# Last attention layer of a four-layer kernel: the sums of squares of a block's later queries and keys share one turn of a PSUM bank, and the next queries are loaded once theirs are stored

## The chip, the cores and the metric

One core of one Trainium2 chip runs the whole program. The metric is the time of one execution in device microseconds (us). Engines are named as in the profile: PE is TensorE (PEld its weight loads), ACT is ScalarE, DVE is VectorE, POOL is GpSimd, SP is SyncE, which in this kernel issues the DMA transfers.

## The reference, cut to what matters

```python
x = A_x                                   # 2048 tokens x 512
x = x + attention(layernorm(x), A_wqkv, A_wo, window of 256)   # layer 0
x = x + attention(layernorm(x), B_wqkv, B_wo, all keys)        # layer 1
x = x + attention(layernorm(x), A_wqkv, A_wo, window of 256)   # layer 2
x = x + attention(layernorm(x), B_wqkv, B_wo, all keys)        # layer 3
# attention: 32 heads of 16; softmax(q k^T / 4) v, heads joined, times wo
```

The words `attention` and `layernorm` stand for the reference's own functions. Layers 1 and 3 are full attention: every query sees all 2048 keys.

## The kernel before, in words

**Pieces.** Tokens are cut into four chunks `c` of 512 queries, heads into eight groups `qd` of four heads, and into four head tiles `t` of eight heads (two groups each). In layer 3 the outer loop is over `t`, then `c`; one pair (t, c) is called a block here, and a block has the two head groups `qd` = 2t and 2t+1. For each head group there are 16 steps `j`, one for each 128 keys (`attn_full`). So a block has 32 steps, and the layer 4 x 4 x 32 = 512.

**A step.** PE makes two score tiles `s` (128 keys x two heads x 512 queries, line 767), ACT takes the exponential of each into a tile `e` (line 771), and PE multiplies `e` with the values into the bank `acc[0]` (line 821), two steps later (`flush(2)`). There are three score banks in layers 1 and 3 (`ps_s` has two, `third` is the other). So PE can be at most three exponentials ahead of ACT.

**Order on PE.** PE's instructions run in the order in which the program writes them. Between the steps the program deals out side work (class `Side`, function `share`): a model clock `clock`, a budget per step, and `PH["free"]`, the model time before which no side work may start, decide how many matmuls of side work follow a step. The order on the other queues is made by the scheduler from when data are expected; SP too takes its instructions strictly in its order, and a waiting one holds up those behind it.

**Side work of layer 3.** It is dealt by blocks (`side3`): in block (t, c) the queries of the next chunk for the same head tile, `Q3(c+1, t)`, then the keys of this chunk for the next head tile, `K3(c, t+1)`; parts of the values (`upper`) before these for t below 2, and parts of the output projection (`O3`) behind them, which for c below 3 there are only in t = 2 and, without a `K3`, in t = 3. With c = 3 come `K3`, then the key shift and `Q3(0, t+1)`. All side work accumulates in one bank, `acc[1]` (function `bank`).

**The sums of squares.** Softmax is kept in range by a shift made of the squared lengths of queries and keys. After a projection (`project`) the squares `sq` of the low-precision result `sp` are made on POOL, and PE sums them over a head's 16 rows with one matmul by `hsum` (line 582, 32 rows of `acc[1]`: rows 32t to 32t+31, `quarters`). For queries DVE scales the sums into `m` (line 611), SP stores `m` into row 3 of each head's rows in the DRAM tensor `qs` (line 617), and only then can the group's query tile `qt` be loaded from `qs` (`load_q`, line 782), since that load reads the row too. For keys DVE takes a maximum into `km` (line 598). Both endings are put on the list `pend`, and `settle()` runs all that stand there. Before: every unit of side work, before its first matmul, settles what is pending and then puts `PH["free"]` 1.6 us ahead (`mms`, lines 386 to 389). At a block's end the rest is settled (line 1089).

**The loads.** A head group needs `qt` (256 KB) and two halves of the keys `kt` (512 KB each, three buffers). Within a block the second group is loaded at the first one's start. The next block's first group is loaded at the start of this block's last group if its `Q3` is done by then (lines 1060 to 1063), otherwise when the next block starts; the scheduler then moves the issues on SP forward to where their data and buffers are expected.

## Time and profile before

| | |
|---|---|
| median of 3 runs | 2648.05 us (2645.96 to 2651.32) |
| the profiled execution | 2648.76 us, its span 2647.0 us |
| PE busy | 2578.7 us, 97% of the span |
| ACT busy | 2384.4 us, 90% |
| DVE, POOL busy | 848.5 us (32%), 583.1 us (22%) |
| layer 3, stretch of its 1024 exponentials | 944.9 us |
| granted PE clock over the span | 0.996 |

A row of groups names the line, the engine, the operation, what it writes and reads, the shape and the count; behind the bar come the busy time, the mean length of one in ns, and the idle time of the engine ahead of them with what ended it. A row of the timeline gives the start, the length, the engine, the line and the count of like instructions in a row; where these have other engines' work between them, the length is from the first start to the last end. In a row of windows, after the stretch and its length, come busy time and count of each engine, then the granted PE clock, the DMA share and GB/s. Busy lengths overlap: an exponential is recorded from its start in the queue, so its own length can be more than the distance to the next one.

### The profile page before, as it was taken

The page shows a single profiled execution, that of the slowest core. Times are in us where ns is not written, and L with a number is a line of the kernel's source. Part 1 is how long each engine was busy: PE and PEld are TensorE (multiplying, and loading weights), DVE is VectorE, ACT ScalarE, POOL GpSimd, SP SyncE. Part 2 cuts the span into 40 slices and gives each one's busy share as a digit, 9 for nine tenths or more (in the row PEclk, how much of TensorE's full clock was granted, in tenths as well). Part 3 has the DMA queues.
Part 4 walks back from the last instruction along what each step waited for, and adds up shares of the span by engine and source line. Part 5 has one row for each costly group of instructions (what it writes and reads, how often), then busy time and mean ns, then how long its engine had stood idle before and what let it go on. Part 6 is the DMA issues. An engine that isn't in the chain of part 4 may idle for free.

```text
span 2647.0 us, 63239 instructions
## 1 busy us (share of the span) xinstructions
PE 2578.7 (97%) x26201; PEld 773.2 (29%) x26201; DVE 848.5 (32%) x1947; ACT 2384.4 (90%) x2725; POOL 583.1 (22%) x1215
## 2 busy tenths in 40 slices
PE   8999999999999999999999999999999999999998
PEld 3333344322222222222223444422222222222222
DVE  5746653112232223112216666211111111222222
ACT  5777665999999999999997787699999999999997
POOL 1889760000000000000006788000000000000000
PEclk9999999999999999999999999999999999999999
DMA  6878766223242234222425655423222233334543
GB/s 203 203 234 266 212 187 186 62 95 124 99 110 91 92 115 123 76 70 88 140 69 161 210 155 158 147 77 94 83 77 69 78 114 99 112 113 139 169 139 116
DMA packets 293185, 341.34 MB, mean 129 GB/s; under 512 B 105928, under 2 KB 199592, under 8 KB 288280
## 3 DMA queue, kind: packets, MB, share of 16 engines
q1 hardware_dynamic: 284376, 310.17, 38.9%
q0 software_dynamic: 8512, 27.04, 3.7%
q8 instruction: 207, 3.39, 0.5%
q14 instruction: 90, 0.74, 0.1%
HBM read 226.49 MB, written 96.99 MB: 122 GB/s over the span
## 4 chain that ended last, share of the span: by engine, by line
PE 86%; ACT 5%; DVE 4%; issue 2%; POOL 1%; DMA 1%; SPq 0%; ACTq 0%; DVEq 0%
PE acc L821 35%; PE s L767 23%; PE acc L395 11%; PE b L398 7%; PE acc L855 5%; ACT e L771 5%; PE b L395 3%; PE bs L398 2%; DVE ot L729 1%; POOL e L844 1%; POOL e L847 0%; DMA x<-in_A_x_dram 0%; DVE xh L462 0%; DVE xh L471 0%; DVE sp L558 0%
## 5 line engine op out<-in xcount | busy, mean ns | idle before, releaser
L771 ACT ACTIVATE e<-s 128x1024 f32<-128x1024 f32 (+2 forms) x2432 | 2246.4, 1086 | 104.5 <-PE s L767 89.6
L821 PE MATMUL acc<-e,vt 128*17 128x512 f32 x8192 | 1078.4, 598 | 4.9 <-DVE ot L729 3.6
L767 PE MATMUL s<-qt,kt 64*128 64x512 f16 (+3 forms) x5440 | 749.8, 354 | 21.4 <-ACT e L771 10.8
L767 PEld LDWEIGHTS <-kt 64*128 64x128 f16 x5440 | 191.1, 94 | 696.3 <-issue 679.3
L821 PEld LDWEIGHTS acc<-e,vt 128*17 128x17 f32 x8192 | 136.4, 95 | 394.7 <-issue 361.7
L729 DVE STREAM_TRANSPOSE ot<-acc 128x512 f32<-128x512 f32 x128 | 91.5, 715 | 496.2 <-PE acc L821 392.3
L847 POOL TENSOR_SCALAR_AFFINE_SELECT e<-e 128x256 f32<-128x256 f32 x512 | 233.6, 464 | 73.7 <-ACT e L771 72.6
L844 POOL TENSOR_SCALAR_AFFINE_SELECT e<-e 128x256 f32<-128x256 f32 x448 | 196.6, 446 | 42.2 <-ACT e L771 39.0
L855 PE MATMUL acc<-e,vt 128*17 128x384 f32 (+2 forms) x2816 | 197.5, 390 | 0.6 <-POOL e L844 0.5
L398 PE MATMUL b<-xc,w 128*128 128x512 f16 x520 | 125.4, 386 | 6.7 <-DMA xc<-xh 4.1
L671 DVE COPY vt<-acc 128x256 f32<-128x256 f32 (+1 forms) x48 | 23.6, 492 | 335.5 <-PE acc L395 335.5
L395 PE MATMUL acc<-wv,xc 128*32 128x256 f16 (+1 forms) x2304 | 120.6, 299 | 0.1
L395 PEld LDWEIGHTS <-xc 128*32 128x32 f16 x2688 | 77.0, 97 | 137.7 <-issue 132.9
L751 POOL TENSOR_TENSOR oh<-o,oh 128x512 f16<-128x512 f32 x19 | 22.1, 1162 | 432.0 <-DVE oh L750 428.8
L676 POOL TENSOR_SCALAR vt<-vt 128x16 f32<-128x16 f32 (+1 forms) x48 | 11.2, 233 | 462.9 <-DVE vt L671 462.7
L395 PE MATMUL acc<-xc,w 128*32 128x512 f16 x1344 | 107.9, 379 | 0.0
L395 PE MATMUL acc<-xc,w_h 128*32 128x512 f16 x1296 | 107.7, 379 | 0.0
L563 POOL TENSOR_TENSOR sq_h<-sp_h 128x512 bf16<-128x512 f16 x27 | 28.1, 1041 | 356.4 <-DVE sp_h L557 295.5
L563 POOL TENSOR_TENSOR sq<-sp 128x512 bf16<-128x512 f16 x28 | 29.2, 1041 | 349.0 <-DVE sp L557 349.0
L557 DVE TENSOR_SCALAR sp<-acc 128x512 f16<-128x512 f32 x28 | 19.4, 692 | 242.3 <-PE acc L395 242.3
L712 DVE SCALAR_TENSOR_TENSOR x<-acc,x 128x512 f32<-128x512 f32 x60 | 41.4, 690 | 169.4 <-PE acc L395 163.4
L395 PEld LDWEIGHTS <-w 128*32 128x32 f16 x1920 | 56.0, 97 | 115.3 <-issue 101.9
(165 smaller groups left out, 1749.4 us busy)
## 6 DMA issues: line engine op xcount, KB each, us to landing
kt<-kf SPq DMA_DIRECT2D x126, 512.0 KB
xd<-x SPq DMA_DIRECT2D x96, 256.0 KB
qt<-qs SPq DMA_DIRECT2D x96, 256.0 KB
x<-xd SPq DMA_DIRECT2D x96, 256.0 KB
w<-wd SPq DMA_DIRECT2D x16, 1024.0 KB
qs<-sp SPq DMA_DIRECT2D x48, 256.0 KB
wv<-wd SPq DMA_DIRECT2D x20, 512.0 KB
x<-in_A_x_dram SPq DMA_DIRECT2D x32, 256.0 KB
```

The costliest lines, as they stand in the source:

```text
L395: nc.tensor.matmul(ps[g:g + 32], a[:, g:g + 32], b, start=(i == 0), stop=(i == len(pairs) - 1), skip_group_check=True)
L398: nc.tensor.matmul(ps, a, b, start=(go and i == 0), stop=(i == len(pairs) - 1))
L563: nc.gpsimd.tensor_tensor(sq, sp[:, 0], sp[:, 0], ALU.mult)
L671: LAST["DVE"] = nc.vector.tensor_copy(to, fr).ins
L712: nc.vector.scalar_tensor_tensor(xs[i], ps, 1.0 / (UP[2] * UP[3]), xs[i], op0=ALU.mult, op1=ALU.add)
L729: nc.vector.transpose(ot.rearrange("p b r -> p (b r)"), a)
L767: nc.tensor.matmul(ps[:, h, s0:s0 + wd_], kt[R * h:R * h + R, pr, kc:kc + P], qt[R * h:R * h + R, pr, qc:qc + wd_], start=True, stop=True)
L771: LAST["ACT"] = nc.scalar.activation(e[:, :, w0:w1], ps[:, :, w0:w1], AF.Exp, scale=SCALE).ins
L821: nc.tensor.matmul(a[32 * h:32 * h + DH + 1, :], V[l, qd // 4, j // 8][:, j % 8, 4 * (qd % 4) + h, :], es_[h // 2][:, h % 2, :], start=(j ...
L844: last = nc.gpsimd.affine_select(v, v, pattern=[[0, 2], [-1, P]], compare_op=ALU.is_gt, fill=0.0, base=0, channel_multiplier=1)
L847: last = nc.gpsimd.affine_select(v, v, pattern=[[0, 2], [1, P]], compare_op=ALU.is_ge, fill=0.0, base=0, channel_multiplier=-1)
L855: nc.tensor.matmul(a[32 * h:32 * h + DH + 1, q * P:(q + nb) * P], V[l, (4 * c + j) // 4][:, j % 4, 4 * qd + h, :], es_[h // 2][:, h % 2, s ...
```

## The change

- `mms` no longer settles when exactly one ending is pending and it belongs to another head tile than the unit that is about to start (`hold`). So the endings of `Q3(c+1, t)` wait, `K3(c, t+1)` runs, and both are settled together: by the next unit of side work, or, where the block has none, at the block's end.
- Where nothing was pending ahead of such a unit, the model holds the next side work back by 1.5 instead of 2.2 after it.
- In the full layers `project` no longer settles by itself after its matmuls.
- The load of the next block's first group is no longer tried only once, at the start of the block's last group, with a forced settling; it is tried after each step of that group, and made when the queries are done and their ending is no longer pending. If that does not happen within the block, it is made when the next block starts, as before.

```diff
-    def mms(ps, pairs, after=1.45, us=MM, go=True):
+    def mms(ps, pairs, after=1.45, us=MM, go=True, hold=None):
...
-        if PH["full"] and pend:
+        if PH["full"] and pend and not (len(pend) == 1 and hold is not None and pend[0][3] not in (None, hold)):
             settle()
             PH["free"] = clock[0] + 1.6
             yield 0.1
...
                 ps = bank()
-                yield from mms(ps, [(w[:, k, a, w0:w0 + P], xc[:, b, k, :]) for k in range(NC) for a, b in TERMS], 2.2)
-            settle(not sqs)
+                yield from mms(ps, [(w[:, k, a, w0:w0 + P], xc[:, b, k, :]) for k in range(NC) for a, b in TERMS],
+                               1.5 if PH["full"] and ht is not None and not pend else 2.2, hold=ht)
+            if not PH["full"]:
+                settle(not sqs)
...
-        pend.append((clock[0] + 3.6, rest, None))
+        pend.append((clock[0] + 3.6, rest, None, ht))
...
-        pend.append((clock[0] + 3.6, rest, ("Q", l, c)))
+        pend.append((clock[0] + 3.6, rest, ("Q", l, c), ht))
...
-                    nxt = None
+                    nxt = following = None
                     if qd + 1 in qds:
                         nxt = load(l, c, qd + 1)
                     elif l == 3:
-                        b, u = (c + 1, t) if c + 1 < NQ else (0, t + 1)
-                        if u < NHT and ("Q3", b, u) in DONE and (b or ("H", u) in DONE):
-                            settle()
-                            loaded[b, 2 * u] = load(l, b, 2 * u)
+                        following = (c + 1, t) if c + 1 < NQ else (0, t + 1)
                     elif c + 1 < NQ and ("Q", l, c + 1) in DONE and (l == 1 or ("K", l, c + 1) in DONE):
-                        if any(f == ("Q", l, c + 1) for _, _, f in pend):
+                        if any(f[2] == ("Q", l, c + 1) for f in pend):
                             settle()
                         loaded[c + 1, qds[0]] = load(l, c + 1, qds[0])
...
                         sd.step()
+                        if following is not None:
+                            b, u = following
+                            if u < NHT and ("Q3", b, u) in DONE and (b or ("H", u) in DONE) and not any(f[2] == ("Q", 3, b) for f in pend):
+                                loaded[b, 2 * u] = load(l, b, 2 * u)
+                                following = None
```

What this does to the order of instructions shows first on PE in the first block of layer 3 (t = 0, c = 0). In a name such as `sq3_0_1_h0` stand the layer, 0 for queries or 1 for keys, the chunk and the head tile; in `e3_0_1_13` layer, chunk, head group and step; in `kt3_1_0_0` and `qt3_1_0` layer, chunk and head group (and the half). The last number is only a running one. Before, the squares of the next chunk's queries are summed in the middle of the second head group, behind the value products of its step 3:

```order
L821 MATMUL acc0_81<-e3_0_1_3_0_23157,vt3_0_0_21822 17x512 x2
L821 MATMUL acc0_81<-e3_0_1_3_1_23162,vt3_0_0_21822 17x512 x2
L582 LDWEIGHTS hsum_86
L582 MATMUL acc1_82<-sq3_0_1_h0_0_23175,hsum_86 32x512
L767 LDWEIGHTS kt3_0_1_0_22648
L767 MATMUL s3_0_1_6_0_23209<-qt3_0_1_22646,kt3_0_1_0_22648 128x512
```

Now they stand at the block's very end, with those of the keys, and the next PE instruction is the first score matmul of the next block, which reads the `qt` of these very queries (line numbers are those of the changed kernel, up to four higher):

```order
L823 MATMUL acc0_81<-e3_0_1_13_0_23358,vt3_0_1_22568 17x512 x2
L823 MATMUL acc0_81<-e3_0_1_13_1_23363,vt3_0_1_22568 17x512 x2
L584 LDWEIGHTS hsum_86
L584 MATMUL acc1_82<-sq3_0_1_h0_0_23175,hsum_86 32x512
L584 LDWEIGHTS hsum_86
L584 MATMUL acc1_82<-sq3_1_0_h1_1_23338,hsum_86 32x512
L769 LDWEIGHTS kt3_1_0_0_23406
L769 MATMUL s3_22643<-qt3_1_0_23404,kt3_1_0_0_23406 128x512
```

So the queries' sums moved from ten steps ahead of the block's end to its end. The same holds for the blocks with c = 0, 1, 2 of t = 0 and t = 1, six in all: there no unit of side work follows `K3` within the block. With t = 2 the two sums stand together in step 3 of the second group (ahead of `O3`), and in the other blocks they move by a step at most.

On SP, at the same place, the rows before are these; `m3_1_0` is the store of the shift row and `qt3_1_0` the load of the next block's queries, `kt3_1_1_0` a half of the keys for the next block's second group:

```order
L571 DMA qs1_1_102<-sp3_0_1_h0_0_23172 128x1024
L572 DMA qs1_1_102<-sp3_0_1_h0_0_23172 128x512
L617 DMA qs1_1_102<-m3_1_0_23206 8x512
L782 DMA qt3_1_0_23404<-qs1_1_102 128x2x512
L792 DMA kt3_1_0_1_23408<-kf_96 128x2x1024
L782 DMA qt3_1_1_23410<-qs1_1_102 128x2x512
L361 DMA wv3_0_1_0_23386<-wd1_2_111 128x8x256
L568 DMA kf_96<-sp3_1_0_h1_1_23339 128x2x512
L569 DMA kf_96<-sp3_1_0_h1_1_23339 128x512
L792 DMA kt3_1_1_0_23412<-kf_96 128x2x1024
```

And now:

```order
L573 DMA qs1_1_102<-sp3_0_1_h0_0_23172 128x1024
L574 DMA qs1_1_102<-sp3_0_1_h0_0_23172 128x512
L794 DMA kt3_1_0_1_23408<-kf_96 128x2x1024
L361 DMA wv3_0_1_0_23382<-wd1_2_111 128x8x256
L570 DMA kf_96<-sp3_1_0_h1_1_23335 128x2x512
L571 DMA kf_96<-sp3_1_0_h1_1_23335 128x512
L794 DMA kt3_1_1_0_23412<-kf_96 128x2x1024
L619 DMA qs1_1_102<-m3_1_0_23399 8x512
L784 DMA qt3_1_0_23404<-qs1_1_102 128x2x512
L784 DMA qt3_1_1_23410<-qs1_1_102 128x2x512
```

The store of `m` and the load of `qt` moved behind `kt3_1_1_0`, whose buffer is given up only by the last score matmuls of the block.

## The prediction, made before the changed kernel was run

> **What bounds the kernel now.** The change acts in layer 3 alone, so I read that stage first. The windows view of the stretch in which its exponentials run, one row for all engines, and the groups of that stretch:

> ```profile
> 1690.00:2625.00 935.00, 927.42 (x9057) 233.09 (x9060) 173.88 (x382) 932.88 (x1014) 50.09 (x62) 1.00 0.34 106
> L771 ACT ACTIVATE e<-s 128x1024 f32<-128x1024 f32 x1014 | 933.6, 1166 | 2.1 <-PE s L767 1.4
> ```

> The first number behind the length is PE, the fourth ACT. ACT is busy 932.9 of 935 us and its idle time in front of 1014 exponentials adds up to 2.1 us; PE is busy 927.4. Both are full, and ACT is the bound. How fast ACT can go shows in a stretch where nothing holds it, against the whole layer (the windows view, ACT's line 771 alone):

> ```profile
> 1924.66:2071.32 146.66, 146.66 (x161) 1.00 0.24 71
> 1687.10:2632.00 944.90, 942.73 (x1024) 1.00 0.34 105
> ```

> 160 exponentials (one of the 161 is cut by the edge) take 146.66 us, 0.917 us each. 1024 of them make 939 us; the layer takes 944.9. So whatever the change does to the order of side work, it can win at most about 6 us, and whatever keeps ACT without scores is lost one for one, since there is no slack to win it back.

> **What the change adds.** In six blocks the store of `m` and the load of `qt` now begin with sums of squares at the block's end, and the next PE instruction needs that `qt`. Before, they stood eight to twelve steps, 15 to 22 us, ahead of that end. The timeline before at such an end (first block):

> ```profile
> 1744.32 0.92 PE L767 MATMUL s<-qt,kt 64*128 64x512 f16 x4
> 1744.85 0.09 PEld L767 LDWEIGHTS <-kt 64*128 64x128 f16 x1 [0.42 <-issue]
> 1745.27 0.36 SPq L792 DMA_DIRECT2D kt<-kf  x1
> 1746.04 0.38 PE L582 MATMUL acc<-sq_h,hsum 128*32 128x512 bf16 x1
> 1746.35 0.39 PE L767 MATMUL s<-qt,kt 64*128 64x512 f16 x2
> ```

> The last two score tiles of the block are made from 1744.32; the second begins at about 1744.85, when ACT has given up a bank. With three banks ACT then has three exponentials left, 3 x 0.917 = 2.75 us, to 1747.60. The sums of squares stand at 1746.04. So from their start ACT is covered for 1.56 us. The squares' start is my zero below.

> How long the chain from squares to scores takes shows once in the trace, at the start of layer 3, where PE does wait for a `qt` (timeline):

> ```profile
> 1679.62 0.39 PE L582 MATMUL bs<-sq_h,hsum 128*32 128x512 bf16 x1
> 1680.05 0.68 DVE L611 TENSOR_SCALAR m<-bs 32x512 f16<-32x512 f32 x1 [1.74 <-PE bs L582]
> 1680.81 0.32 SPq L617 DMA_DIRECT2D qs<-m  x1
> 1683.73 0.37 SPq L782 DMA_DIRECT2D qt<-qs  x1
> 1686.60 0.82 PE L767 MATMUL s<-qt,ke 64*128 64x512 f16 x6 [0.82 <-DMA qt<-qs]
> 1687.09 5.60 ACT L771 ACTIVATE e<-s 128x1024 f32<-128x1024 f32 x6 [0.63 <-PE s L767]
> ```

> Squares to DVE 0.43, DVE 0.68, to the store's issue 0.08, `qt`'s issue to the score matmul 2.87, to the exponential 0.49. Between the two issues there stood other SP work here, so the store is better read elsewhere (SP's own rows, two places):

> ```profile
> 1728.59 0.29 SPq L617 DMA_DIRECT2D qs<-m  x1
> 1730.02 0.38 SPq L782 DMA_DIRECT2D qt<-qs  x1
> ...
> 1789.35 0.34 SPq L571 DMA_DIRECT2D qs<-sp_h  x1
> 1789.74 0.42 SPq L572 DMA_DIRECT2D qs<-sp_h  x1
> 1790.26 0.44 SPq L792 DMA_DIRECT2D kt<-kf  x1
> 1791.85 0.29 SPq L617 DMA_DIRECT2D qs<-m  x1
> 1794.60 0.89 SPq L782 DMA_DIRECT2D qt<-qs  x2
> ```

> Alone it takes 1.43 us until `qt` can be issued; with two `sp` stores and a 512 KB `kt` issued in the 2.5 us ahead, 2.75. In the changed order a `kt` stands right ahead of the store (0.77 us ahead of the squares, by the rows 1745.27 and 1746.04, so some 2 us ahead of the store), but no `sp` store is near. I take 1.8, nearer to the lone one, and keep 1.43 and 2.75 as ends.

> The chain: 0.43 + 0.68 + 0.08 + 1.8 + 2.87 = 5.86 us (5.49 to 6.81). ACT stands idle from 1.56 to 5.86 + 0.49, that is 4.79 us, and the first string after an idle time is 0.1 us longer (six exponentials in 5.60 against 6 x 0.917 = 5.50). **4.9 us per block end, six of them: 29.3 us** (27.1 to 35.0). The second group of squares reads no such chain; its wait for DVE to read the bank lies inside the gap, and so does the load of the second `qt`.

> **What PE does after such a gap.** PE idles from the second sums to 5.86, some 4 us. What that does to its clock shows at two places in the windows view (columns as above; behind the five engines stands the granted clock) and in the chain of waits:

> ```profile
> 300.00:304.00 4.00, 0.52 (x8) 0.00 (x0) 3.90 (x9) 0.26 (x1) 3.99 (x8) 0.93 1.08 341
> 304.00:307.00 3.00, 2.37 (x6) 0.87 (x7) 1.39 (x3) 0.00 (x0) 1.85 (x4) 0.50 1.05 430
> 330.90:334.30 3.40, 1.48 (x22) 0.66 (x24) 3.30 (x6) 0.24 (x1) 0.00 (x0) 1.00 0.62 237
> 334.40:337.60 3.20, 3.20 (x23) 1.44 (x14) 2.25 (x6) 2.12 (x3) 3.11 (x7) 0.50 0.70 181
> 368.50:371.80 3.30, 1.59 (x16) 0.65 (x19) 3.23 (x9) 1.09 (x3) 1.32 (x2) 1.00 1.01 206
> 371.90:375.30 3.40, 3.40 (x37) 1.26 (x33) 1.10 (x4) 2.36 (x4) 2.21 (x6) 1.00 0.98 270
> ```

> ```profile
> 304.63 5.28 PE b L398 x12
> 311.71 2.70 PE b L398 x12
> ```

> After 3.5 idle us of 4 the clock was 0.50, and twelve matmuls took 5.28 instead of 2.70. A stretch of 3.4 us in which PE was busy 1.48 (44%) was followed by about 3.2 us at half clock, one with 1.59 of 3.3 (48%) was not. In the new gap PE has 0.4 us of work in 4, so each gap should bring such a slow stretch. How much of it falls behind the gap depends on how the 3.4 us stretches lie: from 1.5 to 3.4 us, I take 2.8. PE loses half of it, 1.4 us, and since PE has no slack beside ACT (927 of 935), ACT loses it too: **6 x 1.4 = 8.4 us** (0 to 10.2).

> [...]

> **What it moves elsewhere.** In the three blocks of t = 2 both sums stand in the middle, and the second waits for DVE to have read the first (0.43 + 0.68 = 1.1 us). PE is up to three exponentials ahead there, so the wait is mostly covered: I take 0.5 each, 1.5 us (0 to 3.3). The loads there follow at once, some 12 steps ahead of their use: nothing. Some steps that stood empty of side work now hold some, since fewer pauses of 1.6 model us are made. Their price is bounded by the 6 us between 939 and 944.9, below nothing; most of it belongs to places the change leaves (the layer's start, the steps after a new group), and I take -1. What moved by one step in the other blocks costs nothing: the same matmuls run, covered by a full ACT.

> **Sum.** 29.3 + 8.4 + 1.5 - 1 = 38 us, on the profiled execution's 2648.8 (span 2647.0, 0.7 above the median of the runs shown): **2687 us**.

> **Rivals.**
> - *Half clock does not come, or seldom.* For it: at 368.5 a stretch with 1.7 idle us of 3.3 left the clock at 1.00. Against it: the new gaps are more than twice as long. Without the term: 2687 - 8.4 = 2679. Chance 0.2. [...]
> - *The keys' transfer holds the store and the queries.* `kt` is 512 KB on the same queue, and the 2.75 us above was measured behind one. Then the chain is 6.81 us, the stall 5.84, six times 0.95 more: 2693. `qt` too may land late behind it, which I bound by as much again: 2699. Chance 0.13.
> - *The wait is covered, and the fuller steps win.* This one ends on the other side. If the queries of the six ends were in place by the time ACT has used up its three tiles, nothing of the chain would count, and what is left is the gain of up to 6 us: 2643 to 2648. It decides where the chain is under 1.56 - 0.49, about 1.1 us. Against it: the load alone took 2.87. It would need the load to be issued ahead of the block's end, as in t = 2, and the SP rows of the changed order show it behind `kt3_1_1_0`. That the change does less than it says (loads "when stored") is in this order too: stored late, the queries are loaded late. Chance 0.03.

> **Numbers.** The forecast has 0.64. Its own bounds are 27.1 + 6 + 0 - 3, with 2678, to 35.0 + 10.2 + 3.3, with 2697. To hold 8 in 10 the range takes in the first two rivals, less one end of each: 2674 to 2699. A measurement of this kernel can tell about 0.2%, 5 us, from no change: slower 0.97, the same 0.02, faster 0.01 (the last two share the third rival's chance, which lies mostly within 5 us).

> **What the changed profile would show.** Six idle times of ACT of 4 to 6 us ahead of line 771 (its idle time in this stretch 25 to 40 us instead of 2.1), put down to PE's line 767; PE's line 767 waiting for the DMA of `qt` six times; at each, squares, `m`, its store, `kt` ahead of it, `qt` in this order; the granted clock at 0.50 for about 3 us after each; the blocks' other stretches still at 0.917 us per exponential. It is wrong if `qt` is issued ahead of the last score matmuls of the block, if ACT's idle time stays below 10 us, or if the lost time lies in other blocks than these six.

## The result, and the profile after

The change makes the kernel slower: 2694.38 us median (2691.19 to 2695.85, six runs) against 2648.89 us (2644.59 to 2651.32, six runs) of the kernel before, a ratio of 1.0172 (95% interval 1.0161 to 1.0182). That is 45.5 us more, where the forecast said 38. The profiled spans are 2693.3 and 2647.0 us, 46.3 apart. Line numbers below are those of the changed kernel; the exponentials of line 771 now have line 773, the scores of 767 have 769.

The layer first. The windows view of the changed kernel, ACT's exponentials alone, over the stretch that answers to the row of 944.90 us before, then their group:

```profile
1687.20:2678.30 991.10, 947.01 (x1024) 0.99 0.33 101
```

```profile
L773 ACT ACTIVATE e<-s 128x1024 f32<-128x1024 f32 x1019 | 942.4, 1128 | 44.0 <-PE s L769 42.9
```

All of the 46 us is here: 991.1 against 944.9. ACT's idle time ahead of the exponentials rose from 2.1 to 44.0 us. In the waits view of the changed kernel (who waits for whom, us in total, times, longest) the first row is ACT's, and three rows of PE stand behind it:

```profile
ACT e L773 <- PE s L769: 42.9, 35, 4.8
PE s L769 <- DMA qt<-qs: 23.7, 6, 4.1
PE acc L584 <- DVE m L613: 7.0, 9, 0.8
PE acc L584 <- POOL sq_h L565: 3.5, 9, 0.4
```

PE waits six times for a `qt`, 4 us each, once at each of the six block ends. The list before had no such row. At the first of these ends the timeline of the changed kernel shows the chain (start, length, engine; SPq is an issue of SP):

```profile
1744.34 0.92 PE L769 MATMUL s<-qt,kt 64*128 64x512 f16 x4
1745.29 0.36 SPq L794 DMA_DIRECT2D kt<-kf  x1
1746.06 0.38 PE L584 MATMUL acc<-sq_h,hsum 128*32 128x512 bf16 x1
1746.48 0.68 DVE L613 TENSOR_SCALAR m<-acc 32x512 f16<-32x512 f32 x1 [5.41 <-PE acc L584]
1747.18 0.30 SPq L619 DMA_DIRECT2D qs<-m  x1
1747.21 0.39 PE L584 MATMUL acc<-sq_h,hsum 128*32 128x512 bf16 x1 [0.77 <-DVE m L613]
1748.78 0.87 SPq L784 DMA_DIRECT2D qt<-qs  x2
1751.52 1.03 PE L769 MATMUL s<-qt,kt 64*128 64x512 f16 x4 [3.92 <-DMA qt<-qs]
1752.22 1.94 ACT L773 ACTIVATE e<-s 128x1024 f32<-128x1024 f32 x2 [4.66 <-PE s L769]
1752.48 1.91 PE L823 MATMUL acc<-e,vt 128*17 128x512 f32 x8
1755.67 1.02 ACT L773 ACTIVATE e<-s 128x1024 f32<-128x1024 f32 x1 [1.51 <-PE s L769]
```

From the squares at 1746.06 to the scores at 1751.52 it takes 5.46 us: 0.42 to DVE, 0.68 on DVE, 0.02 to the store's issue, 1.60 from there to the issue of `qt`, 2.74 from there to the first score matmul; over the six ends it is 5.40 to 5.65. ACT stands 4.66 us, starts, does two exponentials, and stands again for 1.51 us at 1755.67. That second idle time is the half clock's, as keep_busy shows below. The windows view on PE's own slow stretches at two ends (busy time and count of PE, PEld, DVE, ACT, POOL, then the granted clock):

```profile
1747.39:1750.80 3.41, 0.21 (x1) 0.00 (x0) 0.68 (x1) 0.17 (x1) 0.00 (x0) 0.98 0.48 163
1750.80:1754.22 3.42, 2.71 (x16) 0.53 (x20) 0.00 (x0) 1.94 (x2) 0.00 (x0) 0.50 0.26 91
1754.20:1757.40 3.20, 3.20 (x28) 0.75 (x24) 0.00 (x0) 1.73 (x2) 0.00 (x0) 0.50 0.00 0
1757.60:1761.00 3.40, 3.40 (x54) 1.14 (x50) 2.81 (x8) 2.24 (x4) 0.15 (x1) 1.00 0.01 2
...
1815.65:1819.06 3.41, 0.00 (x0) 0.00 (x0) 0.58 (x1) 0.00 (x0) 0.00 (x0) 0.99 0.48 163
1819.06:1822.47 3.41, 2.95 (x20) 0.65 (x20) 0.00 (x0) 1.94 (x2) 0.00 (x0) 0.51 0.15 53
1822.50:1825.80 3.30, 3.30 (x44) 0.95 (x40) 1.47 (x6) 2.52 (x3) 0.00 (x0) 1.00 0.00 0
```

After the idle stretch at the first end the clock is 0.50 for 6.8 us, at the second for 3.4. Over the six ends it is 6.8 us twice and 3.4 us four times.

How much each place costs shows when the layer is cut into pieces of 32 exponentials (one block and head group: 16 steps of two), from the end of one piece's last exponential to that of the next. In the trace before, the 32 pieces take between 29.3 (32 x 0.917) and 30.3 us, and the first one, from its first start, 30.9. The six pieces that begin with a new block behind the six ends, in us:

| piece | before | after | more |
|---|---|---|---|
| t 0, c 1, first group | 29.33 | 36.98 | 7.65 |
| t 0, c 2 | 29.33 | 35.52 | 6.19 |
| t 0, c 3 | 29.33 | 36.56 | 7.23 |
| t 1, c 1 | 29.33 | 35.93 | 6.60 |
| t 1, c 2 | 29.33 | 35.61 | 6.28 |
| t 1, c 3 | 29.50 | 37.05 | 7.55 |

They hold 41.5 of the 46.2 us; 4.7 lie in other pieces.

### The profile page after: what moved, and what is told of

Its sections match the earlier page's. It is cut to its first block, busy times and chain, and to the rows that moved or that the text cites. A ratio compares the mean times of both kernels' runs of the same rounds, so it can differ in the third digit from the quotient of the medians.

```text
span 2693.3 us, 63244 instructions
## 1 busy us (share of the span) xinstructions
PE 2592.3 (96%) x26201; PEld 772.2 (29%) x26201; DVE 845.5 (31%) x1947; ACT 2389.3 (89%) x2725; POOL 583.1 (22%) x1215
## 4 chain that ended last, share of the span: by engine, by line
PE 84%; ACT 5%; DVE 5%; issue 2%; DMA 2%; POOL 1%; SPq 0%; ACTq 0%; DVEq 0%
PE acc L823 34%; PE s L769 22%; PE acc L395 11%; PE b L398 7%; PE acc L857 5%; ACT e L773 5%; PE b L395 3%; PE bs L398 2%; DMA qt<-qs 1%; DVE ot L731 1%; DMA xc<-xh 0%; DMA qs<-m 0%; POOL sq_h L565 0%; DMA x<-in_A_x_dram 0%; DVE sp_h L559 0%
## 5 line engine op out<-in xcount | busy, mean ns | idle before, releaser
L398 PE MATMUL b<-xc,w 128*128 128x512 f16 x520 | 125.3, 386 | 5.5 <-DVE oh L752 4.3
```

The costliest lines, as they stand in the source:

```text
L398: nc.tensor.matmul(ps, a, b, start=(go and i == 0), stop=(i == len(pairs) - 1))
```

## The experiments

Each is an edit of the changed kernel. Ratios are to the kernel before, run on the same chip. Its medians were 2647.15 us beside half_dose, hold_alone, keep_busy and sums_earlier, 2648.37 beside load_alone, keys_behind, pause_2_2 and middle_alone, and 2649.48 beside queries_first and middle_both_first; it was 2648.89 beside the changed kernel.

**half_dose: the deferred ending at three ends instead of six.** The queries' ending waits only for keys of head tile 1, that is in t = 0; everything else settles as before, and the model's pause is 2.2 as before.

```diff
-                               1.5 if PH["full"] and ht is not None and not pend else 2.2, hold=ht)
+                               2.2, hold=ht if ht == 1 and s == 1 else None)
```

> Only the three block ends of t = 0 keep the shared turn; all other blocks settle as before the change. If the time is lost in the chain from squares to the next block's first scores (theory A), three of the six ends remain, which cost 7.65, 6.19 and 7.23 us in the profile after: before + 21, about 2670 us. If it is lost by the new spread of the side work and the waits around the shared bank in all of the layer (theory B), the loss follows the changed blocks of all four head tiles and three of them leave about a quarter: about 2660 us.

2665.75 us, 1.0073 (1.0056 to 1.0089). The waits view of this kernel:

```profile
ACT e L773 <- PE s L769: 20.6, 13, 4.8
PE s L769 <- DMA qt<-qs: 11.8, 3, 4.0
```

The layer is 20.4 us longer than before, and the three pieces behind the three ends are longer by 7.58, 6.26 and 6.49, 20.3 us together; the three ends of t = 1 are at 29.33, 29.33 and 29.50 again. The total fell between the two expectations, so it is the pieces that decide: the loss sits at the ends, 6.8 us each, and goes where they go.

**hold_alone: the load tried once, as before, the ending deferred.** The new retry after each step is taken out.

```diff
-                        following = (c + 1, t) if c + 1 < NQ else (0, t + 1)
+                        b, u = (c + 1, t) if c + 1 < NQ else (0, t + 1)
+                        if u < NHT and ("Q3", b, u) in DONE and (b or ("H", u) in DONE) and not any(f[2] == ("Q", 3, b) for f in pend):
+                            loaded[b, 2 * u] = load(l, b, 2 * u)
```

> The shared turn without the repeated try of the load: the load of the next block's first group is tried once, at the start of the last group, and not while its ending is pending. Theory A: the six ends stay as they are, since there the ending is pending to the block's end in either form: 2694 us, within 3. If the repeated try had a part in it (the load placed badly), the time moves by more than 5 us.

2695.91 us, 1.0183 (1.0166 to 1.02): the whole of the loss, without the changed load.

**load_alone: the other half, the new load with the endings settled as before.**

```diff
-                               1.5 if PH["full"] and ht is not None and not pend else 2.2, hold=ht)
+                               2.2)
```

> The repeated try of the load without the shared turn (every unit settles what is pending, as before). PE's order is that of the kernel before. Theory A: no loss, 2649 us within 3. If the place from which the load is made matters, a few us either way.

2647.79 us, 0.9999 (0.9989 to 1.001). The pause is 2.2 here too, and pause_2_2 below keeps nearly the whole loss with that pause and the later ending. So the later ending is the cause; the rule for the load neither costs nor wins by itself.

**keep_busy: PE kept at work in the gap.** At the six ends PE is given 14 matmuls of constants into a part of the bank that nothing reads; the result doesn't use them.

```diff
+WARM = 14
...
                 if not win:
+                    idle = len(pend) == 2
                     settle()
+                    if idle:
+                        for _ in range(WARM):
+                            nc.tensor.matmul(acc[1][96:128], ones[:, :32], ones, start=True, stop=True, skip_group_check=True)
```

> The changed kernel with 14 more matmuls behind the shared sums at each of the six ends, into 32 rows of the second bank that nothing reads; they fill PE's gap from about 2.3 to 5.3 us behind the squares and add no work that the result uses. If the half clock behind the gap costs ACT about 2 us per end, the granted clock stays at 1.00 and the time falls by 10 to 13 us, to about 2682. If the slow stretch is covered and the loss is the chain alone, nothing changes: 2694, or a little more where the extra matmuls end late.

2684.08 us, 1.0142 (1.0125 to 1.0159): 10 us under the changed kernel by the medians, 8 by the ratios. Its timeline at the first end, then the windows view behind it:

```profile
1746.42 3.18 PE L1098 MATMUL acc<-ones 128*32 128x512 f16 x14 [0.77 <-DVE km L601]
1746.74 0.87 SPq L785 DMA_DIRECT2D qt<-qs  x2
1749.53 0.60 PE L770 MATMUL s<-qt,kt 64*128 64x512 f16 x4
1750.02 1.94 ACT L774 ACTIVATE e<-s 128x1024 f32<-128x1024 f32 x2 [4.41 <-PE s L770]
1750.07 1.05 PE L824 MATMUL acc<-e,vt 128*17 128x512 f32 x8
```

```profile
1749.50:1752.90 3.40, 3.40 (x43) 1.06 (x45) 0.00 (x0) 2.88 (x4) 0.00 (x0) 1.00 0.03 9
```

The chain is as long as ever (`qt`'s issue to the scores 2.79 us), ACT still stands 4.41 us, but the clock stays at 1.00; eight value products take 1.05 us instead of 1.91, and the second idle time is 0.19 us instead of 1.51. The six pieces are now 31.3 us longer than before instead of 41.5. The half clock is worth 10.2 us in this pair of traces, 1.7 per end, and what is left is 5.2 per end: 4.7 to 4.9 at the four ends with c = 1 and 2, 5.9 and 6.1 at the two with c = 3.

**sums_earlier: the queries' ending settled inside the block**, near the time at which the model expects the keys' squares; the keys' ending stays at the block's end. The queries' sums come out one step (1.8 us) ahead of the keys' at two ends and two steps (3.7 us) at four.

```diff
                             b, u = following
+                            if b and len(pend) == 2 and pend[-1][0] - 2.0 <= clock[0]:
+                                settle(True, 1)
+                                PH["free"] = clock[0] + 1.6
```

> The queries' sums are made one step (two ends) or two steps (four ends) ahead of the block's end, the keys' sums stay there; on SP the store goes ahead of the keys' transfer, the load of the queries stays behind it and so waits for the last score matmuls. Theory A: the load is issued about 0.3 us ahead of my zero instead of 2.7 behind it, so each end costs 2 to 3 us instead of 6.9: 2664 to 2670 us. Theory B, which puts the loss in the bank and the spread of the side work: these have not changed, so about 2694.

2690.93 us, 1.0168 (1.0151 to 1.0185): a miss. In this trace the layer starts 1.63 us earlier than in the changed kernel's (1685.62 against 1687.25). Counted from that start, the sums of the first end come 1.83 us earlier, the scores only 0.71. Its timeline at the first end:

```profile
1742.60 0.38 PE L584 MATMUL acc<-sq_h,hsum 128*32 128x512 bf16 x1
1743.72 0.30 SPq L619 DMA_DIRECT2D qs<-m  x1
1744.11 0.37 SPq L794 DMA_DIRECT2D kt<-kf  x1
1745.04 0.88 SPq L784 DMA_DIRECT2D qt<-qs  x2
1749.18 1.04 PE L769 MATMUL s<-qt,kt 64*128 64x512 f16 x4 [4.36 <-DMA qt<-qs]
1749.88 1.94 ACT L773 ACTIVATE e<-s 128x1024 f32<-128x1024 f32 x2 [3.94 <-PE s L769]
```

The 512 KB `kt`, whose buffer the last score matmuls free at about 1744, now goes out between the store and `qt`, and the scores come 4.14 us after `qt`'s issue instead of 2.74. At the four ends with two steps the order costs more. There `kt` waits for that buffer, and `qt`, behind it on SP, is issued 2.2 us after the store (1.3 at the first end); the scores then come 4.4 to 4.7 us after `qt`'s issue. The next two kernels test that reading.

**keys_behind: `kt` issued behind `qt`**, in the changed kernel's own place for the sums.

```diff
-        nc.sync.dma_start(qt, qs[1, c][2 * qd:2 * qd + 2].rearrange("r p n -> p r n"))
+        LQ[qd] = nc.sync.dma_start(qt, qs[1, c][2 * qd:2 * qd + 2].rearrange("r p n -> p r n")).ins
...
+            with tc.issue_after(LQ[qd - 1]) if l == 3 and qd % 2 and qd < 4 else nullcontext():
                 nc.sync.dma_start(kt, kf[pair, :, v * S // 2:(v + 1) * S // 2].rearrange("r p n -> p r n"))
```

> The changed kernel with the transfer of the next block's second keys held on SP until the queries' load is issued, for t = 0 and t = 1. The store of the shift row then has the queue to itself: 1.3 instead of 1.6 us to its landing. If the transfer ahead of it delays the chain by just that, each end gains 0.3 us: about 2692. If it also delays the queries, 0.5 to 1 each: 2688 to 2691.

2694.46 us, 1.0164 (1.0149 to 1.018), which the time can't tell from the changed kernel. In the timeline the store's issue is 1.32 us ahead of `qt`'s instead of 1.60:

```profile
1747.53 0.30 SPq L619 DMA_DIRECT2D qs<-m  x1
1748.85 0.88 SPq L784 DMA_DIRECT2D qt<-qs  x2
1749.77 0.46 SPq L797 DMA_DIRECT2D kt<-kf  x1
1751.64 1.04 PE L769 MATMUL s<-qt,kt 64*128 64x512 f16 x4 [3.69 <-DMA qt<-qs]
```

The six pieces together are 1.5 us shorter than with `kt` ahead. In the changed kernel, where `kt` goes 1.9 us ahead of the store, the keys' transfer holds the chain by 0.3 us per end and no more.

**queries_first: the last two together**, the queries' sums inside the block and `kt` behind `qt`; the edit is that of sums_earlier and that of keys_behind.

> The kernel with the earlier sums (one step at two ends, two steps at four), and the keys' transfer held on SP until the queries' load is issued. In the run with earlier sums alone the load was issued 0.93 us behind that transfer and took 4.1 us to the scores instead of 2.7. If the transfer ahead was what ate the steps won, the chain is 5.4 us from the squares again, so scores come 3.5 us behind my zero at two ends and 1.7 at four: idle times of 2.5 and 0.7 us, and with half clock at the two 8 to 11 us in all, beside the 4 to 5 us in other blocks: 2661 to 2666 us. If the queries land as late as before, 2691.

2666.59 us, 1.0059 (1.0044 to 1.0075), just above the expected range. Its timeline at the first end:

```profile
1743.60 0.38 PE L584 MATMUL acc<-sq_h,hsum 128*32 128x512 bf16 x1
1744.72 0.30 SPq L619 DMA_DIRECT2D qs<-m  x1
1746.04 0.88 SPq L784 DMA_DIRECT2D qt<-qs  x2
1746.97 0.46 SPq L797 DMA_DIRECT2D kt<-kf  x1
1749.05 0.61 PE L769 MATMUL s<-qt,kt 64*128 64x512 f16 x4 [3.22 <-DMA qt<-qs]
1749.53 1.03 ACT L773 ACTIVATE e<-s 128x1024 f32<-128x1024 f32 x1 [2.59 <-PE s L769]
```

`qt` to scores is 3.01 us, and the chain is 5.45 us, as in the changed kernel; it only starts earlier. ACT's waits for scores add up to 14.6 us instead of 42.9. Beside sums_earlier (2690.93 us) it shows that the order of `kt` and `qt` on SP's queue is worth 24 us once the sums come earlier: the layer takes 986.5 us with the one, 962.8 with the other. From the sums to the scores it takes 6.6 us at two ends and 7.8 to 8.1 at four with `kt` ahead, and 5.2 to 5.5 with it behind; and half clock follows at one end in place of six (granted clock of the profiled run 0.995, against 0.991 in the changed kernel).

A wait remains, since the chain starts one or two steps earlier and not its whole length. ACT's idle times are 2.6 and 2.5 us at two ends and 0.6 to 0.7 at four, as forecast. The six pieces are 13.2 us longer than before, where 8 to 11 were expected.

**pause_2_2: the model's pause after a unit left at 2.2** instead of 1.5, the deferred ending as in the change.

```diff
-                               1.5 if PH["full"] and ht is not None and not pend else 2.2, hold=ht)
+                               2.2, hold=ht)
```

> The changed kernel with the model's pause behind a unit at 2.2 everywhere, as before the change. Theory A: the six ends keep their cost; what the profile after shows beside them (PE waiting for POOL's squares and for DVE in the blocks with c = 3 and in t = 3, some 2 to 3 us) goes: about 2691 us. If the shorter pause costs nothing, 2694.

2691.70 us, 1.0156 (1.014 to 1.0172); the interval overlaps that of the changed kernel, so the time leaves it open. The waits view of this kernel answers to the row of 3.5 us, nine times, in the changed one:

```profile
PE acc L584 <- POOL sq_h L565: 0.4, 1, 0.4
```

The pieces with c = 3 or in t = 3, which the change had made 2.4 us longer together, are back to within 0.02 us of before. The gain doesn't reach the total: behind this kernel's six ends eleven stretches of 3.4 us are recorded at half clock instead of eight, and these six pieces are 2.1 us longer than in the changed kernel. hold_alone has eleven too, and its six pieces are 3.3 us longer. The granted clocks of the profiled runs are 0.990 and 0.989, against 0.991 in the changed kernel. So the half clock's price differs from trace to trace.

**middle_alone: only what the change does in t = 2**, where the two endings meet in the middle of a block.

```diff
-                               1.5 if PH["full"] and ht is not None and not pend else 2.2, hold=ht)
+                               2.2, hold=ht if ht == 3 and s == 1 else None)
```

> Only the blocks of t = 2 share the turn, where it is followed by a unit of the output projection in the same block and the queries are loaded a dozen steps early. Theory A: no chain at a block's end, so only the second sum's wait for DVE: 0.5 to 1 us in each of three blocks, 2650 to 2652 us. Theory B: a share of the 45 us, at least 8: 2657 or more.

2650.11 us, 1.0004 (0.9994 to 1.0013): the time can't be told from that of the kernel before. In the trace the layer is 2.4 us longer. In the timeline, the place in the second block of t = 2:

```profile
2257.72 0.38 PE L584 MATMUL acc<-sq_h,hsum 128*32 128x512 bf16 x1
2258.89 0.39 PE L584 MATMUL acc<-sq_h,hsum 128*32 128x512 bf16 x1 [0.78 <-DVE m L613]
```

**middle_both_first: the same, with both sums ahead of both reads.** The two matmuls write different rows of the bank; here the pending entry carries its matmul apart, so that the second is written before DVE's read of the first. The edit is cut to the place that settles:

```diff
+        if PH["full"] and len(pend) == 2:
+            both = [(p, p[4]()) for p in pend]
+            pend.clear()
+            for p, ph in both:
+                p[1](ph)
```

> The kernel that shares the turn only in t = 2, with both matmuls by hsum ahead of both reads of the bank by DVE, so that the second does not wait for the first one's read. If that wait is what made those blocks 0.6 to 0.9 us longer, they come back to 29.3 us and the kernel to 2648 us, not more than 1 us from before. If the squares on POOL or the stretch behind set it, nothing changes: 2650.

2648.92 us, 0.9996 (0.9987 to 1.0005). The same place in its timeline, two matmuls in a row:

```profile
2255.81 0.39 PE L584 MATMUL acc<-sq_h,hsum 128*32 128x512 bf16 x2
```

The second groups of c = 0, 1, 2 in t = 2 are at 30.05, 29.34 and 29.33 us (middle_alone 30.67, 30.28, 30.28; before 30.09, 29.34, 29.33). The wait of 0.78 us on PE cost ACT 0.6 to 0.95 each. This is the whole idea of the change at the places where it does no harm, and it ties with the kernel before. No kernel here beats that one by more than can be measured.

## Why the prediction was right, point by point

**ACT is the bound and nothing is won back.** Right. The pieces away from the ends stay at 29.3 to 30.9 us, and ACT's new idle time, 42 us, is the new time but for some 4 us.

**The chain from squares to scores.** Predicted 5.86 us, measured 5.46. The uncertain term, store to issue of `qt`, was taken at 1.8 between 1.43 and 2.75 and is 1.60 behind a `kt` and 1.3 without one near (keys_behind, queries_first). ACT's idle time was predicted at 4.79 and is 4.66: only 0.13 less, because the step from scores to exponential is longer at half clock (0.70, against 0.49 in keep_busy). The stall alone was predicted at 4.9; by keep_busy it is 4.7 to 4.9 at the four ends with c = 1 and 2. At the two with c = 3 something else is added (see the shorter pause below).

**The half clock behind the gap.** It came at all six ends, and keep_busy shows its price: 10.2 us, where 8.4 was predicted and 10.2 was the upper bound. That it stayed within the bound was partly luck: with the eleven slow stretches of hold_alone the same difference is 13.5 us. The mis-sized part is the slow time behind each gap, taken as 2.8 us: counted from the scores it is 2.8 to 6.0 us, 3.7 in the mean, since two ends have two slow stretches. The rival without it, 2679, fell.

The prediction's row with 1.48 busy us, a partly idle stretch with half clock behind it, carried over to the new gaps: in the changed kernel's trace, of the six stretches of 3.41 us ahead of a slow one two held no PE work, the other four 0.07 to 1.55 us.

**What moves elsewhere: the step that failed in size.** The prediction put 1.5 us on the second sums' wait in t = 2, -1 on fuller steps, and nothing on "what moved by one step in the other blocks", +0.5 in all. The pieces outside the six say +4.7. The second groups of t = 2 with c below 3 are 2.1 us longer, within the bounds, and middle_both_first shows that it is that wait. The pieces with c = 3 or in t = 3 are 2.4 us longer, and there the shorter pause was overlooked: with 1.5 instead of 2.2 PE comes to the sums before POOL has the squares (nine waits, 3.5 us). pause_2_2 takes that away. The second group of the second block (t 0, c 1) is 0.8 us longer, and the same kernel takes 0.5 of it away; the cause of the rest stays open. Of the gain from fuller steps, 0.6 us can be seen in two pieces (t 2, c 0, first group, 0.44; t 0, c 0, second group, 0.14), not 1.

The shorter pause also reaches into the two ends with c = 3. With one slow stretch each they take 36.56 us (t 0) and 37.05 (t 1) in the changed kernel, and with the pause at 2.2 35.82 (half_dose) and 36.41 (pause_2_2). So some 1.4 of the 41.5 us belong to it, an estimate from these four pieces.

**The sum.** 41.5 at the six ends (37.7 predicted) and 4.7 elsewhere (0.5 predicted). Both parts were forecast too small, so the two misses add up. The lower bound of the prediction took the half clock at 6 us, though its term went down to 0; the time came out near the upper end, so nothing hangs on that.

**The rivals.** That the keys' transfer holds store and queries: in the changed order it does by 0.3 us per end (keys_behind), not by 1 to 2, with `kt` 1.9 us ahead of the store. The measured 2694 us lies by this rival's 2693, but only the number agrees. The mechanism exists at another place: between the store and `qt` the same transfer makes the chain 1.1 to 2.8 us longer (sums_earlier against queries_first). That the wait is covered: it isn't, with six waits of PE for `qt`.

**What the profile should have shown.** Six ACT idle times of 4 to 6 us: yes. 25 to 40 us of idle time ahead of the exponentials: 44.0, over it by the longer half clock and the waits elsewhere. The clock at 0.50 for about 3 us after each: 3.4 us four times and 6.8 twice. PE waiting six times for `qt`'s DMA, and the order squares, `m`, store, `qt` with `kt` ahead: yes.

## What to carry to other kernels

An ending that feeds a load has to start a whole chain ahead of the load's use, here 5.5 us from the sums through DVE, store and load to the next matmul, and a bounded lead (three banks, 2.75 us) covers only part of it; put late, it cost its uncovered part at every place plus what the idle engine's clock lost after it (5.2 and 1.7 us per end by keep_busy). Before such an ending is moved, look at what else is issued on its DMA queue at the new place: a transfer that was harmless ahead of the pair can take most of what the move wins when it falls between the two (24 of 28 us at the six ends here). When two sums share a bank, write both matmuls before the first read: with the read between them the second waited 0.78 us on PE (middle_alone against middle_both_first).

## What the runs showed of the hardware

**A load behind a large transfer on its queue.** `qt` (256 KB) took 2.74 us from its issue to the scores with the last `kt` (512 KB) issued 3.5 us ahead (first end of the changed kernel), and 4.14 us with it 0.93 us ahead; with it 0.5 us ahead, 4.4 to 4.7 us (both sums_earlier).

**How much idle time it takes.** In queries_first gaps of 3.22 and 3.08 us had different outcomes. The windows view of that kernel, on these steps, behind both:

```profile
1747.01:1750.42 3.41, 1.38 (x12) 0.39 (x16) 0.00 (x0) 0.89 (x1) 0.00 (x0) 1.00 0.88 269
1750.42:1753.83 3.41, 3.41 (x28) 0.82 (x24) 0.00 (x0) 2.88 (x4) 0.00 (x0) 0.50 0.10 39
1811.86:1815.28 3.42, 1.52 (x17) 0.50 (x20) 0.00 (x0) 1.03 (x2) 0.00 (x0) 1.00 0.76 240
1815.28:1818.69 3.41, 3.41 (x48) 0.95 (x41) 1.47 (x6) 3.31 (x4) 0.00 (x0) 1.00 0.18 67
```

A step with 1.38 busy us (40%) was followed by half clock, one with 1.52 (44%) was not. The bound isn't quite sharp: the prediction's row with 1.48 of 3.4 was followed by half clock, and so was this one of the changed kernel, at the first end of t = 1:

```profile
2003.28:2006.70 3.42, 1.55 (x10) 0.23 (x9) 1.37 (x2) 2.29 (x3) 0.00 (x0) 1.00 0.57 156
2006.70:2010.11 3.41, 0.62 (x4) 0.16 (x4) 0.00 (x0) 0.00 (x0) 0.00 (x0) 0.50 0.47 154
```

Both gaps of queries_first are shared by two steps: of the 3.22 us at most 2.03 lie in the step shown, of the 3.08 at most 1.89. So near this length one gap cost a slow stretch and the other nothing. In the traces before and after, from where their clock is recorded on, each of the 12 steps at full clock with up to 1.55 us of PE work was followed by half clock, and so were three of the four with 1.62 to 1.68. The gaps of 3.9 to 4.1 us of the changed kernel all cost a slow stretch. In keys_behind the six waits for `qt` are 3.7 us in the mean and 3.8 at most, and the granted clock of the profiled run is 0.992, against 0.991 in the changed kernel.
